# Cutting some stores of an attention gradient into 120 and 8 rows, and 104 and 24 rows

## The chip, the cores and the metric

The kernel runs on one core of one Trainium2 chip. The metric is device time in microseconds for one execution. The profiled execution has a span, from the first to the last instruction of the program, which is a little shorter than its device time.

A core has TensorE (PE in the profile; PEld is its weight load), VectorE (DVE), ScalarE (ACT), GpSimd (POOL) and SyncE (SP), and 16 DMA engines that move data between HBM and the on-chip memory (SBUF, 128 partitions; a partition is called a row below). POOL's and SP's instruction queues issue the DMAs of this kernel.

## What is computed

The reference is the forward pass of a grouped-query attention and its gradients, for B = 32 batches, 32 query heads, 4 key heads, 4 queries, 2048 keys and a head size of 128, in bf16:

```python
scores = jnp.einsum("bhqd,bhkd->bhqk", q, k) * scale
p = _softmax(scores, axis=-1)
return jnp.einsum("bhqk,bhkd->bhqd", p, v)
...
_out, _vjp = jax.vjp(_f, q, k, v)
_grads = _vjp(grad_out)
```

The four outputs are o, dq, dk and dv. k, v, dk and dv are large: 2 MB each for a batch (4 heads x 2048 x 128 values of 2 bytes). q, grad_out, o and dq have 128 x 128 values a batch (32 heads x 4 queries), 32 KB.

## The kernel before

The kernel goes through the 32 batches one at a time, with several in flight. The order of all steps of all engines is written out by hand: a list HEAD for the first batches, a list STEADY of 48 steps that is repeated, and a list TAIL for the last ones. A step such as `dV3@5` is the third eighth of dV of batch 5.

For a batch b, in the order of the data:

- `LK`, `LV` load k and v, four DMAs each of one head (512 KB), from SP's queue. The 2048 keys of a head lie as 128 rows of 16 keys, so that a row of a head is 4 KB in one piece. Three k buffers and two v buffers rotate. Every fourth batch (b % 4 = 3) `LK` also loads q and grad_out of the next four batches, two DMAs of 128 KB from POOL's queue.
- `KT`, `VT`, `QDT` turn k, v, q and grad_out on PE; DVE copies the result out of PSUM.
- `S`, `EX`, `NRM` make scores, exponentials and 1/sum; POOL writes the scaled copies `dop` and `qp` that dV and dK need (line 231).
- `ET` and `O`: o is accumulated on PE, DVE scales it into `o_sb`, and POOL issues its store of 128 rows x 256 bytes. DVE then reads `o_sb` once more for `delta`.
- `dV0` to `dV7`: outer products on PE, ACT copies each eighth into the tile `dv` (128 rows x 4 heads x 16 keys x 128). With the last eighth POOL issues two stores, two heads and 1 MB each.
- `dP`, `dST`, `dQ`, and `dK0` to `dK7`, which are stored as dV is.

The last batch (b = 31) stores dV and dK in another way, by halves of the keys. POOL issues in its queue's order, for each batch: dq, dk, dk (of the batch before), o, dv, dv, and in every fourth the two loads of q and grad_out. `store` in the code is POOL's queue.

DMAs that are issued by POOL take one of eight semaphores in turn. The trace shows them on semaphores 111 to 118 in rotation, and an issue waits until the store that used the semaphore before it has landed.

In the code of before the store of dV and dK is at line 326 (line 319 for the last batch), that of o at line 276, that of dq at line 290, the loads of q and grad_out at line 142, k's and v's at lines 154 and 160.

Of the kernel before, what the change touches and what calls it, by code (L numbers as in the profile page):

```python
# [9 lines left out]
BF16 = mybir.dt.bfloat16  # L10
ACT = mybir.ActivationFunctionType
ALU = mybir.AluOpType
# [69 lines left out]
def kernel(ctx: ExitStack, tc: tile.TileContext, q, k, v, grad_out, out_0, out_1, out_2, out_3):  # L82
    nc = tc.nc
    B, Hq, Sq, D = q.shape
    NH, Sk = k.shape[1], k.shape[2]
    P = 128
# [3 lines left out]
    scale = float(D) ** -0.5  # L90
# [11 lines left out]
    ds_pool = ctx.enter_context(tc.tile_pool(name="dsp", bufs=2))  # L102
    dst_pool = ctx.enter_context(tc.tile_pool(name="dstp", bufs=2))
    out_pool = ctx.enter_context(tc.tile_pool(name="outp", bufs=4))
    io_pool = ctx.enter_context(tc.tile_pool(name="iop", bufs=3))
    qd_pool = ctx.enter_context(tc.tile_pool(name="qdp", bufs=2))
    sm_pool = ctx.enter_context(tc.tile_pool(name="smp", bufs=3))
    ps_pool = ctx.enter_context(tc.tile_pool(name="ps", bufs=1, space=bass.MemoryType.PSUM))
# [16 lines left out]
    o_f = out_0.rearrange("b h s d -> b (h s) d")  # L125
# [6 lines left out]
    store = nc.gpsimd  # L132
    st = {}
# [125 lines left out]
    def gathered(S, xt, kv):  # L259
        t = banks.take(1)  # L260
        ps = banks.ap(t)[:, 0, 0:D]
        for c in range(C):
            for h in range(NH):
                nc.tensor.matmul(  # L264
                    ps[G * h:G * h + G, :], lhsT=S[f"{xt}{c // 8}"][:, c % 8, G * h:G * h + G], rhs=S[kv][:, h, c, :],
                    start=(c == 0), stop=(c == C - 1), tile_position=(0, G * h),
                )
        return t, ps

    def O(b):  # L270
        S = st[b]
        t, ps = gathered(S, "et", "v")
        o_sb = io_pool.tile([P, D], BF16, name="o_sb")
        nc.vector.tensor_scalar(out=o_sb[:], in0=ps, scalar1=S["rinv"][:], scalar2=None, op0=ALU.mult)
        banks.give(t)
        store.dma_start(out=o_f[b], in_=o_sb[:])
        junk = sm_pool.tile([P, D], BF16, name="junk")
        S["delta"] = sm_pool.tile([P, 1], FP32, name="delta")
        nc.vector.tensor_tensor_reduce(
            out=junk[:], in0=o_sb[:], in1=S["do"], scale=1.0, scalar=0.0,  # L280
            op0=ALU.mult, op1=ALU.add, accum_out=S["delta"][:],
        )

# [8 lines left out]
    def outer(S, x, y, dst, name, i, b, copy):  # L292

        if name not in S:
            S[name + "left"] = 8
            S[name] = out_pool.tile([P, NH, C, D], BF16, name=name, tag="outp")
        t = banks.take(2)
        ps = banks.ap(t).rearrange("p a (j c d) -> p a j c d", j=2, c=2)
        for c in range(2):
            u = P * ((2 * i + c) % 8)  # L300
            for a in range(2):
                r = slice(2 * G * a, 2 * G * a + 2 * G)
                nc.tensor.matmul(  # L303
                    ps[:, a, :, c, :], lhsT=S[f"{x}{i // 4}"][r, u:u + P], rhs=S[y][r, :, :],
                    start=True, stop=True, tile_position=(2 * G * a, 0),
                )
        copy(  # L307
            out=S[name][:, :, 2 * i:2 * i + 2, :].rearrange("p h c d -> p h (c d)"),
            in_=banks.ap(t).rearrange("p a (j w) -> p (a j) w", j=2),
        )  # L310
        banks.give(t)
        S[name + "left"] -= 1
        if b == B - 1:

            half = f"{name}half{i // 4}"
            S[half] = S.get(half, 4) - 1
            if S[half] == 0:
                c = slice(8 * (i // 4), 8 * (i // 4) + 8)
                store.dma_start(
                    out=dst[b].rearrange("p h (c d) -> p h c d", d=D)[:, :, c, :].rearrange("p h c d -> p h (c d)"),  # L320
                    in_=S[name][:, :, c, :].rearrange("p h c d -> p h (c d)"),
                )
        elif S[name + "left"] == 0:
            o = S.pop(name)
            for a in range(2):
                store.dma_start(out=dst[b][:, 2 * a:2 * a + 2, :], in_=o[:, 2 * a:2 * a + 2].rearrange("p h c d -> p h (c d)"))  # L326

    def dV(b, i, copy=nc.scalar.copy):
        outer(st[b], "e", "dop", dv_v, "dv", i, b, copy)

    def dK(b, i, copy=nc.scalar.copy):
        outer(st[b], "ds", "qp", dk_v, "dk", i, b, copy)

    def dP(b, i):
# [6 lines left out]
        banks.give(t)  # L341

    table = {"LK": LK, "LV": LV, "QDT": QDT, "O": O, "dQ": dQ, "NRM": NRM}
    for i, c in enumerate("ab"):
        for n, f in (("S", S_), ("EX", EX), ("dP", dP), ("ET", ET), ("dST", dST)):
# [8 lines left out]
    for w in STEADY.split():  # L354
        ahead = 0
        for mark, n in (("+3", 3), ("+2", 2), ("+", 1), ("-2", -2), ("-", -1)):
            if w.endswith(mark):
                w, ahead = w[:-len(mark)], n
# [3 lines left out]
    with tc.manual_schedule():  # L362

        for w in HEAD.split():
            w, b = w.split("@")
# [5 lines left out]
        for w in TAIL.split():  # L371
            w, b = w.split("@")
# [31 lines left out]
```

## Time and profile before

| what | value |
|---|---|
| median of 3 runs | 700.39 us (700.14, 700.39, 703.01) |
| profiled execution | 698.71 us |
| its span | 696.7 us |
| granted TensorE clock, mean | 0.980 |
| PE, DVE, ACT, POOL busy | 90%, 84%, 82%, 43% of the span |
| DMA packets | 75577, 274.44 MB, 394 GB/s over the span |
| POOL's DMA queue (q0), SP's (q1) | 138.16 MB, 134.50 MB |
| issue to landing, median: k, v, dv, dk | 13.8, 18.6, 23.6, 22.1 us |

The DMA share in the profile is the time that packets took, over 16 engines' time. Issue to landing counts from the issuing instruction to the last completion that the transfer sends. A wait in the profile is idle time of an engine, put down to what ended it.

### The profile page before, as it was taken

The numbers are of one execution on the slowest core, as the hardware profiler recorded it, in microseconds if no ns is written. First come the engines' busy times: TensorE is split into PE (matmuls) and PEld (weight loads), VectorE is DVE, ScalarE is ACT, GpSimd is POOL, SyncE is SP. The second block draws the span as 40 slices with busy tenths as digits, with TensorE's granted clock in tenths as the row PEclk, the third lists the DMA queues.
The fourth block names the chain that finished last, engine by engine and source line by source line (L and its number), as shares of the span: only waits on it lengthen the run. The fifth ranks groups of instructions, "written<-read, shape, count | busy, mean of one in ns | idle before, by whom it ended". The sixth has DMA issues, their size and how long they took to land.

```text
span 696.7 us, 28064 instructions
## 1 busy us (share of the span) xinstructions
PE 626.0 (90%) x12352; PEld 454.1 (65%) x12352; DVE 584.5 (84%) x992; ACT 569.1 (82%) x673; POOL 302.7 (43%) x506
## 2 busy tenths in 40 slices
PE   5899999999998989979999798998998889998982
PEld 4577776677676656666666676667766677666661
DVE  5999999999997998869988688888988869898960
ACT  0698989899887989869888687887888868888994
POOL 1355443555454435443354424544434543345452
PEclk9999999999999999999999899999999989999997
DMA  9989999999999999999999999999999999999767
GB/s 339 400 317 411 417 415 416 416 413 415 417 415 417 414 417 416 417 409 412 415 415 413 373 397 398 400 410 382 416 416 417 415 340 393 415 414 415 289 257 274
DMA packets 75577, 274.44 MB, mean 394 GB/s; under 512 B 8448, under 2 KB 8448, under 8 KB 75456
## 3 DMA queue, kind: packets, MB, share of 16 engines
q0 software_dynamic: 37536, 138.16, 49.3%
q1 hardware_dynamic: 37920, 134.50, 48.9%
q8 instruction: 96, 1.57, 0.8%
q14 instruction: 25, 0.20, 0.1%
HBM read 136.31 MB, written 136.31 MB: 391 GB/s over the span
## 4 chain that ended last, share of the span: by engine, by line
PE 43%; DMA 33%; ACT 6%; DVE 5%; POOL 5%; issue 5%; SPq 0%; POOLq 0%; DVEq 0%; ACTq 0%
PE banks L181 18%; DMA k_sb<-in_k_dram 15%; DMA out_dram<-dk 12%; PE banks L303 10%; PE banks L264 7%; ACT dv L307 5%; PE banks L248 5%; DMA out_dram<-dv 4%; PE banks L198 3%; POOL dop L231 2%; DMA v_sb<-in_v_dram 2%; DVE kt L183 2%; DVE ds L338 1%; ACT dk L307 1%; POOL qp L231 1%
## 5 line engine op out<-in xcount | busy, mean ns | idle before, releaser
L307 ACT CAST dv<-banks 128x1024 bf16<-128x1024 f32 x256 | 245.5, 1028 | 56.9 <-PE banks L303 56.3
L307 ACT CAST dk<-banks 128x1024 bf16<-128x1024 f32 x256 | 250.7, 1025 | 34.5 <-PE banks L303 23.6
L183 DVE COPY kt<-banks 128x1024 bf16<-128x1024 bf16 x256 | 164.3, 680 | 8.3 <-PE banks L181 8.3
L183 DVE COPY vt<-banks 128x1024 bf16<-128x1024 bf16 x256 | 166.2, 680 | 1.3 <-PE banks L181 0.9
L181 PE MATMUL banks<-ident,k_sb 128*128 128x128 bf16 x2048 | 145.8, 221 | 13.1 <-DMA k_sb<-in_k_dram 8.6
L181 PE MATMUL banks<-ident,v_sb 128*128 128x128 bf16 x2048 | 143.5, 220 | 14.3 <-ACT dv L307 9.7
L231 POOL TENSOR_SCALAR dop<-do_sb,rinv 32x128 bf16<-32x128 bf16 x128 | 76.7, 599 | 181.3 <-PE banks L303 118.9
L181 PEld LDWEIGHTS <-k_sb 128*128 128x128 bf16 x2048 | 120.8, 99 | 41.9 <-issue 31.7
L181 PEld LDWEIGHTS <-v_sb 128*128 128x128 bf16 x2048 | 122.2, 98 | 28.7 <-issue 23.3
L303 PE MATMUL banks<-dop,e 64*128 64x256 bf16 x1024 | 99.3, 276 | 15.1 <-POOL dop L231 11.3
L326 POOL DMA_DIRECT2D out_dram<-dv x62 | 43.7, 709 | 138.0 <-ACT dv L307 67.6
L338 DVE SCALAR_TENSOR_TENSOR ds<-banks,delta,e 128x1024 bf16<-128x1024 f32 x64 | 82.2, 1284 | 17.3 <-PE banks L198 14.3
L303 PE MATMUL banks<-qp,ds 64*128 64x256 bf16 x1024 | 86.4, 272 | 2.1 <-ACT dk L307 1.4
L231 POOL TENSOR_SCALAR qp<-q_sb,srinv 32x128 bf16<-32x128 bf16 x128 | 78.1, 610 | 10.7
L222 ACT ACTIVATE e<-banks,negb 128x1024 bf16<-128x1024 f32 x64 | 70.7, 1111 | 8.6 <-DVE negb L214 8.5
L211 DVE TENSOR_REDUCE m<-banks 128x1 f32<-128x1024 f32 x64 | 75.1, 1215 | 0.9 <-PE banks L198 0.9
L303 PEld LDWEIGHTS <-e 64*128 64x128 bf16 x1024 | 34.0, 94 | 63.1 <-issue 46.7
L250 DVE COPY et<-banks 128x1024 bf16<-128x1024 bf16 x64 | 41.3, 686 | 29.6 <-PE banks L248 29.6
L303 PEld LDWEIGHTS <-ds 64*128 64x128 bf16 x1024 | 42.2, 94 | 28.8 <-ACT dv L307 13.1
L326 POOL DMA_DIRECT2D out_dram<-dk x62 | 44.0, 713 | 13.6 <-DMA out_dram<-dk 13.0
L250 DVE COPY dst<-banks 128x1024 bf16<-128x1024 bf16 x64 | 43.5, 681 | 5.5 <-PE banks L248 3.6
L248 PE MATMUL banks<-ident,ds 128*128 128x128 bf16 x512 | 39.4, 221 | 7.1 <-ACT dk L307 6.8
(39 smaller groups left out, 484.1 us busy)
## 6 DMA issues: line engine op xcount, KB each, us to landing
k_sb<-in_k_dram SPq DMA_DIRECT2D x128, 512.0 KB, 13.8
v_sb<-in_v_dram SPq DMA_DIRECT2D x128, 512.0 KB, 18.6
out_dram<-dv POOLq DMA_DIRECT2D x64, 1024.0 KB, 23.6
out_dram<-dk POOLq DMA_DIRECT2D x64, 1024.0 KB, 22.1
out_dram<-o_sb POOLq DMA_DIRECT2D x32, 32.0 KB, 23.2
out_dram<-dq_sb POOLq DMA_DIRECT2D x32, 32.0 KB, 16.2
q_sb<-in_q_dram POOLq DMA_DIRECT2D x7, 128.0 KB, 21.9
do_sb<-in_grad_out_dram POOLq DMA_DIRECT2D x7, 128.0 KB, 22.0
```

Of the source, the lines that this page charges most:

```text
L181: nc.tensor.transpose(out=ps[:, 4 * hh + j, :], in_=S[which][:, 2 * (i % 2) + hh, 4 * (i // 2) + j, :], identity=ident[:])
L183: nc.vector.tensor_copy(out=S[f"{which}t{i}"][:], in_=ps)
L211: nc.vector.reduce_max(out=S["m"][:, i:i + 1], in_=S[f"s{i}"][1], axis=AX.X)
L222: nc.scalar.activation(out=S[f"e{i}"][:], in_=ps, func=ACT.Exp, bias=S["negb"][:], scale=scale, accum_out=S["l"][:, i:i + 1],)
L231: nc.gpsimd.tensor_scalar(out=t[r, h % 2, :], in0=src[r, :], scalar1=by[r, :], scalar2=None, op0=ALU.mult)
L248: nc.tensor.transpose(out=ps[:, u, :], in_=S[f"{src}{i}"][:, P * u:P * u + P], identity=ident[:])
L250: nc.vector.tensor_copy(out=S[f"{name}{i}"][:], in_=ps)
L264: nc.tensor.matmul(ps[G * h:G * h + G, :], lhsT=S[f"{xt}{c // 8}"][:, c % 8, G * h:G * h + G], rhs=S[kv][:, h, c, :], start=(c == 0), stop ...
L303: nc.tensor.matmul(ps[:, a, :, c, :], lhsT=S[f"{x}{i // 4}"][r, u:u + P], rhs=S[y][r, :, :], start=True, stop=True, tile_position=(2 * G * ...
L307: copy(out=S[name][:, :, 2 * i:2 * i + 2, :].rearrange("p h c d -> p h (c d)"), in_=banks.ap(t).rearrange("p a (j w) -> p (a j) w", j=2),)
L326: store.dma_start(out=dst[b][:, 2 * a:2 * a + 2, :], in_=o[:, 2 * a:2 * a + 2].rearrange("p h c d -> p h (c d)"))
L338: nc.vector.scalar_tensor_tensor(out=S[f"ds{i}"][:], in0=ps, scalar=S["delta"][:], in1=S[f"e{i}"][:], op0=ALU.subtract, op1=ALU.mult,)
```

## The change

Two stores are cut differently, and one pool of buffers is smaller.

- dV, second store (heads 2 and 3): in the batches with b % 4 = 3 it becomes two, rows 0 to 119 and rows 120 to 127. In batch 0 it becomes three: rows 0 to 119 of head 2, rows 0 to 119 of head 3, rows 120 to 127 of both. The last batch's dV goes another way through the code and stays as it is. dK is not changed.
- o: two batches share one tile. The first four batches, and those with b % 4 = 0 or 1, are stored as before. A batch with b % 4 = 2 issues no store; with b % 4 = 3 both batches are stored, rows 0 to 103 in one DMA and rows 104 to 127 in another.
- the pool of `o_sb` and `dq_sb` has two buffers each in place of three; `o_sb` is twice as large.

All other steps, and their order, are the same. The bytes moved are the same.

```diff
-    io_pool = ctx.enter_context(tc.tile_pool(name="iop", bufs=3))
+    io_pool = ctx.enter_context(tc.tile_pool(name="iop", bufs=2))
...
-        o_sb = io_pool.tile([P, D], BF16, name="o_sb")
-        nc.vector.tensor_scalar(out=o_sb[:], in0=ps, scalar1=S["rinv"][:], scalar2=None, op0=ALU.mult)
-        banks.give(t)
-        store.dma_start(out=o_f[b], in_=o_sb[:])
+        if b % 2 == 0:
+            st["o"] = io_pool.tile([P, 2, D], BF16, name="o_sb")
+        o_sb = st["o"][:, b % 2, :]
+        nc.vector.tensor_scalar(out=o_sb, in0=ps, scalar1=S["rinv"][:], scalar2=None, op0=ALU.mult)
+        banks.give(t)
+        if b < 4 or b % 4 < 2:
+            store.dma_start(out=o_f[b], in_=o_sb)
+        elif b % 4 == 3:
+            for r in (slice(0, 104), slice(104, P)):
+                store.dma_start(out=o_f[b - 1:b + 1, r].rearrange("w p d -> p w d"), in_=st["o"][r])
...
             o = S.pop(name)
             for a in range(2):
-                store.dma_start(out=dst[b][:, 2 * a:2 * a + 2, :], in_=o[:, 2 * a:2 * a + 2].rearrange("p h c d -> p h (c d)"))
+                parts = [(slice(0, P), slice(2 * a, 2 * a + 2))]
+                if name == "dv" and a and b == 0:
+                    parts = [(slice(0, 120), slice(2, 3)), (slice(0, 120), slice(3, 4)), (slice(120, P), slice(2, 4))]
+                elif name == "dv" and a and b % 4 == 3:
+                    parts = [(slice(0, 120), slice(2, 4)), (slice(120, P), slice(2, 4))]
+                for r, h in parts:
+                    store.dma_start(out=dst[b][r, h, :], in_=o[r, h].rearrange("p h c d -> p h (c d)"))
```

## The prediction

> **What bounds the kernel now.** I read the page's busy rows first, then its DMA queues, then the DMA view of single stretches, last POOL's timeline.
>
> ```profile
> span 696.7 us, 28064 instructions
> ...
> PE 626.0 (90%) x12352; PEld 454.1 (65%) x12352; DVE 584.5 (84%) x992; ACT 569.1 (82%) x673; POOL 302.7 (43%) x506
> ...
> DMA  9989999999999999999999999999999999999767
> GB/s 339 400 317 411 417 415 416 416 413 415 417 415 417 414 417 416 417 409 412 415 415 413 373 397 398 400 410 382 416 416 417 415 340 393 415 414 415 289 257 274
> ```
>
> The DMA engines are full from the third slice to the loads' end, at 409 to 417 GB/s as far as slice 22; then dips to 340 appear. PE's 90% is an average that includes waits. The DMA view gives issues, KB each and the median us from issue to landing; here for 60 to 200 us, and below it for 400 to 640 us:
>
> ```profile
> out_dram<-dk POOLq DMA_DIRECT2D x14, 1024.0 KB, 15.9
> out_dram<-dv POOLq DMA_DIRECT2D x14, 1024.0 KB, 21.1
> ```
>
> ```profile
> out_dram<-dk POOLq DMA_DIRECT2D x24, 1024.0 KB, 23.0
> out_dram<-dv POOLq DMA_DIRECT2D x22, 1024.0 KB, 26.1
> ```
>
> The stores fall further behind although the rate doesn't rise. Why, the completions tell. The trace records sixteen for each transfer, one from each DMA engine. Of the second dk store of batch 4, fifteen are in by 143.04 us and the last at 145.00; of batch 16, by 393.39 and at 403.46; of batch 27, by 627.98 and at 642.57. One engine falls behind steadily (2.0, 10.1, 14.6 us). From batch 4 to 16 its pace is (403.46 - 145.00) / 12 = 21.54 us a batch; that of the fifteenth is (393.39 - 143.04) / 12 = 20.86, the mean of all sixteen 20.76. After batch 16 the fifteen are throttled to the late one, which holds its 21.5. When the loads have ended, it is seen alone. In the DMA view of 654 to 657 us:
>
> ```profile
> DMA  0101001001010101010010101010090101010010
> q0 software_dynamic: 15, 0.06, 5.1%
> q8 instruction: 1, 0.02, 2.9%
> q1 hardware_dynamic: 4, 0.01, 1.2%
> ```
>
> 5.1% + 1.2% of sixteen engines is one engine, still at work while fifteen rest. The seventeen 4 KB packets that it starts from 654.10 to 657.02 us are 0.172 us apart; on the others, when busy, packets follow each 0.155 us (34.58 to 36.15 us). So this lane is slow by itself, not by what it is given: all stores of before have 128 rows. An engine's eight rows of two heads are 16 of these packets.
>
> How the lateness comes back shows on POOL's timeline (start, us, instruction; in brackets the idle time before it and what ended that):
>
> ```profile
> 527.09 1.42 POOL L326 DMA_DIRECT2D out_dram<-dk  x2
> 529.95 0.56 POOL L276 DMA_DIRECT2D out_dram<-o_sb  x1 [1.44 <-DMA out_dram<-dk]
> 534.93 1.40 POOL L326 DMA_DIRECT2D out_dram<-dv  x2 [4.42 <-DMA out_dram<-dk]
> 541.85 2.63 POOL L231 TENSOR_SCALAR dop<-do_sb,rinv 32x128 bf16<-32x128 bf16 x4 [5.51 <-PE banks L303]
> ```
>
> Stores rotate over eight semaphores, so each waits for the eighth before it to land in full, its late engine too. These waits throttle fifteen engines; the late one has 14 us of work queued and never rests. Compute alone would go faster: between 73.0 and 191.5 us, before these waits, dv's first store is issued every 19.75 us.
>
> **The change part by part.** The sum is against the profiled execution: 698.71 us, 2.0 more than its span, 1.7 under the median of the three runs (700.39). I carry its differences to the median.
>
> *The dV store cut into 120 and 8 rows.* The bytes stay. No row of before shows how 120 rows are dealt to sixteen engines. If an engine keeps its eight rows, fifteen take part and one is left out; the 8-row piece then gives that engine one row back or none. It loses 14 to 16 packets. If the rows are spread evenly, it loses next to nothing. Which engine is spared, the trace doesn't say either: it doesn't name engines. So one event is worth, if the late lane is the spared one, 14 x 0.172 = 2.4 us at the pace when alone, or 14 x 0.163 = 2.3 at the pace under load (21.54 us less about 0.7 for o, dq, completions and the q and do loads, over 128 packets); with 16 packets, up to 2.75. If another engine is spared, it is worth 0, or -2 x 0.172 = -0.34 where the late lane takes a row of the 8-row piece. I take 2.3. It happens in batches 3, 7, ..., 27: seven times (batch 31 is stored in another way). From batch 3 on the late lane always has a backlog, so a microsecond less of its work is one less at the end: 7 x 2.3 = 16.1. The cap: at 20.86 a batch the fifteenth lane would end 23 x 0.68 = 15.6 us earlier at batch 27, plus the 2.0 it led by at batch 4, so 17.6 at most. The late lane, at 21.54 - 0.58 = 20.96 a batch, stays just the slowest; the seven rows given away cost others 0.08 a batch.
>
> *Whether it is the same engine each time.* If the pieces are dealt from a pointer that runs on, the 120- and 8-row pieces use 15 + 8 shares, o's 104 and 24 rows 13 x 8 and 12 x 2, so 25. Together 48, three times round sixteen: the pointer stands where it stood, and all seven events spare one engine. The first dV's pieces (15 + 15 + 8 = 38) move it by six places once, ahead of the rest. Dealt from a fixed first engine, it is one engine as well.
>
> [...]
>
> *First dV, batch 0.* At 34 us no lane is behind (the sixteenth completion follows the fifteenth by 0.3 us), so no gain. Two more issues of 0.71 us are followed by an idle POOL: its next store is at 47.3 us. Cost 0.
>
> *o in pairs.* In batch b%4 = 2 the issue (0.56 us) goes, in b%4 = 3 there are two; the store of the even batch moves past two dv, one dq and two dk stores of POOL's queue. Nobody reads o on the chip except DVE, from SBUF. An engine's share is 2 KB of a batch, one packet of 0.08 us; whatever the dealing does, it is under 0.2 us an event, either way. I take 0.
>
> *One more dV issue in every fourth batch.* 0.71 us of POOL in front of the next dop. POOL waits 5.51 us for PE there: hidden. Without that cover it would be 7 x 0.71 = 5.0 us. The wait for the eighth store back is a rival below.
>
> *io pool with two buffers.* dq_sb is written again two batches later, 42 us; its store lands 16.2 us (median) after issue. An o pair is written again four batches later. 0, and a landing over 40 us would be needed for more.
>
> [...] Here the 32 KB o stores already run among full queues at 415 GB/s without a dip.
>
> Sum: 698.71 - 16.1 = 682.6 in a profiled execution, 684.3 in the median.
>
> **Rivals.** *Another engine is spared, or the rows are spread evenly.* For: nothing in the trace ties the late lane to rows 120 to 127. Against: the pieces close on one engine every time, and the late engine is also one and the same throughout. Times: 700.4, or 700.4 + 7 x 0.34 = 702.8 where the late lane takes one of the eight rows. Both are within 0.5% (3.5 us), about what a measurement of this kernel can tell from no change. In this case the change doesn't do what it could.
>
> *Slower: POOL's wait for the eighth store back.* In a batch with b%4 = 3 the order becomes dq, dk, dk, o, o, dv, dv, dv. The last piece then waits for the last dv store of the batch before: in the timeline above that one (issued at 514.4) lands at 545.9, so POOL would be held until then and not until 536.3. dop, ready to start at 541.85, would start 4.8 us late, and PE with its dV. Price without cover: 7 x 4.8 = 33.6, so 734. Against it: compute has (21.5 - 19.75) x 4 = 7 us to spare in four batches, and the late lane keeps its backlog of 14 us. It decides only if the hold in four batches exceeds these 7 us, say by a slow issue of odd pieces on POOL; with 2 us over, 7 x 2 = 14 and 714. If the late lane is relieved, the wait shrinks with the landing.
>
> *No engine has what the late one lost.* If the fifteenth lane becomes the bound early (cap halved), the gain is about 8: 692.
>
> **How the numbers follow.** Late lane spared, in full: 0.47, 680 to 688. Spared but capped: 0.11, 688 to 696. Another engine or even spread: 0.33, 699 to 703.5. POOL's wait: 0.09, 704 and up. The first is a judgement, as the trace doesn't name engines; I put it over the miss because the spared engine is one and the same by the arithmetic, as the late lane is throughout, and because the rows left over are always the last eight. If the two places are unrelated, a hit is one in sixteen and the miss is the answer; that doubt is the 0.33. Faster by over 0.5%: 0.58; within: 0.33; slower: 0.09. Range 680 to 703.5, which leaves out POOL's wait; the likeliest case alone is 680 to 688.
>
> **What would show it.** Right: the sixteenth completion of batch 27's second dk store is a few us behind the fifteenth, not 14.6; landing of dk and dv at 400 to 640 us near 17 to 20 us; POOL's 4.4 us waits gone or shorter; GB/s near 415 with few dips. Miss: the same 14 us and the same landing medians. POOL's wait: three dv issues with a gap of 5 us or more before the last, and dop released by POOL, with PE idle. Wrong altogether: time and landings both move, but no lane's lag does.

## The result, and the profile after

Over twenty runs of each kernel the changed one takes 702.60 us (700.32 to 706.26) and the one before 700.38 (698.19 to 703.40): ratio 1.0031, 95% interval 1.0019 to 1.0042. The change brings nothing and costs some 2 us. The profiled execution of after took 703.15 us, 4.4 more than that of before.

The first fence is the head of the profile page of after: span, DMA share and rate in 40 slices.

```profile
span 701.3 us, 28111 instructions
...
DMA  8999999999999999999999999999999999999867
GB/s 336 398 316 404 414 414 411 415 414 416 415 416 415 411 416 412 414 391 407 414 385 404 403 416 413 358 411 387 400 409 364 408 408 400 396 386 416 337 237 266
```

The dips from the middle of the run on are still there (391, 385, 358, 387, 364). The DMA view of after for 400 to 640 us (issues, KB each, median us from issue to landing) shows the two pieces of dV apart:

```profile
out_dram<-dk POOLq DMA_DIRECT2D x24, 1024.0 KB, 21.5
...
out_dram<-dv POOLq DMA_DIRECT2D x19, 1024.0 KB, 24.4
out_dram<-dv POOLq DMA_DIRECT2D x3, 960.0 KB, 26.5
...
out_dram<-dv POOLq DMA_DIRECT2D x3, 64.0 KB, 21.8
```

dk and dv land 1.5 and 1.7 us sooner than before, not down to the forecast's 17 to 20 us, and a store of 8 rows takes 21.8 us, nearly as long as one of 128. The completions say why. Of the second dk store of batch 27, the sixteenth was in at 642.57 us before and is at 642.50 after: the late engine has been relieved of nothing. The fifteenth moved from 627.98 to 634.52. The lag of the late engine is 8.0 us in place of 14.6 only because the other fifteen are slower; the lag alone would have passed for half a success.

What holds the other fifteen shows in POOL's waits. Three groups of the wait view (engine and line, what it waited for, us in total, times, longest us), of before and then of after:

```profile
POOL dop L231 <- PE banks L303: 118.9, 20, 6.6
POOL out_dram L326 <- DMA out_dram<-dv: 22.1, 6, 4.2
PE banks L303 <- POOL dop L231: 11.3, 11, 2.4
```

```profile
POOL dop L231 <- PE banks L309: 93.5, 19, 6.2
POOL out_dram L340 <- DMA out_dram<-dv: 72.5, 22, 4.5
PE banks L309 <- POOL dop L231: 21.2, 16, 2.9
```

POOL waits 50 us more for landed dv stores and 25 us less for PE; PE waits 10 us more for `dop`. In a batch with the cut, POOL's timeline of after (start, us, instruction; in brackets the idle time before it and what ended it) reads:

```profile
430.62 0.73 POOL L340 DMA_DIRECT2D out_dram<-dv  x1 [4.99 <-DMA out_dram<-dk]
435.17 0.74 POOL L340 DMA_DIRECT2D out_dram<-dv  x1 [3.82 <-DMA out_dram<-dv]
440.44 0.55 POOL L340 DMA_DIRECT2D out_dram<-dv  x1 [4.53 <-DVE vt L183]
441.08 2.63 POOL L231 TENSOR_SCALAR dop<-do_sb,rinv 32x128 bf16<-32x128 bf16 x4
```

Each dv piece now waits on its own, and `dop` follows the last issue with no pause: POOL is no longer waiting for PE there. The stores eight back, on the same semaphores, had their last completions at 430.06, 434.89 and 440.16 us, each 0.3 to 0.6 us before the issue that waited. (DVE's vt as what ended the last wait is a neighbour in time; DVE gives nothing to that store.)

### The profile page after: what moved, and what is told of

Read it like the earlier page. It is cut to its first block, busy times and chain, and to the rows that moved or that the text cites. A ratio compares the mean times of both kernels' runs of the same rounds, so it can differ in the third digit from the quotient of the medians.

```text
span 701.3 us, 28111 instructions
## 1 busy us (share of the span) xinstructions
PE 629.5 (90%) x12352; PEld 457.5 (65%) x12352; DVE 584.0 (83%) x992; ACT 569.4 (81%) x673; POOL 309.8 (44%) x515
## 4 chain that ended last, share of the span: by engine, by line
PE 51%; DMA 23%; issue 8%; ACT 6%; POOL 6%; DVE 4%; SPq 0%; POOLq 0%; ACTq 0%; DVEq 0%
PE banks L181 21%; DMA out_dram<-dv 14%; PE banks L309 13%; PE banks L264 7%; DMA out_dram<-dk 7%; PE banks L248 5%; ACT dv L313 5%; PE banks L198 4%; POOL dop L231 3%; DMA v_sb<-in_v_dram 2%; POOL out_dram L340 2%; DVE kt L183 1%; DVE ds L352 1%; ACT dk L313 1%; DMA k_sb<-in_k_dram 1%
## 5 line engine op out<-in xcount | busy, mean ns | idle before, releaser
L340 POOL DMA_DIRECT2D out_dram<-dv x71 | 49.1, 693 | 176.8 <-ACT dv L313 76.2
L309 PE MATMUL banks<-dop,e 64*128 64x256 bf16 x1024 | 101.2, 277 | 24.8 <-POOL dop L231 21.2
L309 PE MATMUL banks<-qp,ds 64*128 64x256 bf16 x1024 | 88.8, 273 | 2.1 <-ACT dk L313 1.4
L309 PEld LDWEIGHTS <-ds 64*128 64x128 bf16 x1024 | 44.2, 94 | 28.8 <-ACT dv L313 12.7
L276 DVE TENSOR_SCALAR o_sb<-banks,rinv 128x128 bf16<-128x128 f32 x32 | 11.2, 351 | 39.8 <-PE banks L264 39.2
```

The costliest lines, as they stand in the source:

```text
L309: nc.tensor.matmul(ps[:, a, :, c, :], lhsT=S[f"{x}{i // 4}"][r, u:u + P], rhs=S[y][r, :, :], start=True, stop=True, tile_position=(2 * G * ...
L340: store.dma_start(out=dst[b][r, h, :], in_=o[r, h].rearrange("p h c d -> p h (c d)"))
```

## How the dealing can be read

The trace names no engine, but it shows one that is left out: an engine that gets no rows of a POOL store still moves very small packets. Packets of POOL's queue, by size in bytes:

```
before: 4 x3296, 2048 x1024, 4096 x33216
after:  4 x3696, 16 x28, 64 x21, 1024 x84, 2048 x800, 4096 x33307
```

The change adds, in seven pairs of o, 7 x 13 = 91 packets of 4096 bytes and 7 x 3 = 21 of 64 (104 rows on 13 engines, 3 left out), 7 x 12 = 84 of 1024 and 7 x 4 = 28 of 16 (24 rows on 12 engines, 4 left out). So 16 - k engines are left out where a store is dealt to k. For a 120-row dV store the left-out engine shows a chain of sixteen and more 4-byte packets, 5.9 ns apart. In after one of them starts at 437.25 us, while that store's completions run from 437.86 to 461.7: the left-out engine stands at the front, so it is a fast one. The 4-byte packets tell how many are left out there. In before they are as many as the completions on POOL's eight semaphores, 206 x 16 = 3296; after has 215 x 16 = 3440 completions and 256 such packets more. In seven events, 15 engines for 120 rows leave one out, with 16 packets, and 8 for 8 rows leave eight out, with 2 each: 7 x (16 + 8 x 2) = 224, and 224 of the 256 come after 70 us. The other 32 are of batch 0.

When the 64-byte packets of a 104-row store come late, with its last completion, the late engine is among the three left out. Where it lies, and where it doesn't, in kernels with different dealing tells its place. Below, places 0 to 15 are counted from the engine where the program's dealing begins. That a store which is dealt to k engines, k under 16, moves the place where the next such store begins by k is an assumption, which the runs below test, and the turn is the number of places by which batch 0 has moved it. For 104, 24, 120 and 8 rows k is that of the packets above (13, 12, 15 and 8); for the other cuts below (22 rows on 11 engines, say) it is an estimate after these, where the engines that take part get equal rows. Then, as counted, the 120-row store leaves out place (turn + 15) mod 16, and its 8-row piece gives a row of each head to eight places from that one on. The first event leaves the place 15 + 8 = 23 further on, so the 104-row store takes thirteen places from turn + 7 on and leaves out turn + 4, + 5 and + 6. The 24-row store behind it leaves out turn to turn + 3, and its 16-byte packets tell of these four in the same way.

## The experiments

The diffs are against the changed kernel, except where said. The timed ratio is to the kernel before, on the same chip; "late end" is the sixteenth completion of batch 27's second dk store (before 642.57, after 642.50). It is that of one execution: in e3, which stores dV as before, it is 644.28, so differences of less than 2 us say little.

**No cut of the first dV (e1).**

```diff
-                if name == "dv" and a and b == 0:
-                    parts = [(slice(0, 120), slice(2, 3)), (slice(0, 120), slice(3, 4)), (slice(120, P), slice(2, 4))]
-                elif name == "dv" and a and b % 4 == 3:
+                if name == "dv" and a and b % 4 == 3:
```

> The changed kernel without the cut of the first dV store; all else as changed. In the changed kernel's trace the engine that each 120-row store leaves out is one that finishes among the first, and the late lane keeps all its packets (batch 27's second dk store ends at 642.50, before the change at 642.57). Theory A, one running pointer decides which engine is left out and the cut of the first dV only turns it by six places: now another engine is left out, the same in all seven events. If that is the late lane: about 684 us, lag of the sixteenth completion at batch 27 a few us. If it is again another one: 700 to 703, lag 8 to 14 us. Theory B, the engine left out is fixed by the row order and the first dV has no say: 702.6, same lane left out as in the changed kernel.

703.92 us, 1.005 (1.0018 to 1.0083); late end 644.60. A 64-byte packet of a 104-row store comes at 451.08 us with that store's last completion at 451.8, the other fifteen being in by 439.3. Without a turn the late engine is among the three left out there, as counted at place 4, 5 or 6, and it gets a row of each 8-row piece. In after no such packet comes late (for the same pair the last is at 437.10 us, the store's last completion at 451.24): the first dV's pieces do turn the dealing, but not to the right place.

**The same stores, dealt evenly (e2)** (112 and 16 rows for 120 and 8, 64 and 64 for 104 and 24).

```diff
-                parts = [(slice(0, 120), slice(2, 4)), (slice(120, P), slice(2, 4))]
+                parts = [(slice(0, 112), slice(2, 4)), (slice(112, P), slice(2, 4))]
```

> The changed kernel with the same number of stores, cut so that the rows can be dealt evenly over sixteen engines: dV as 112 and 16 rows, o pairs as 64 and 64. Theory A, what the change lost (2.2 us) comes from the extra stores and POOL's waits for the eighth store back: 702 to 703, the wait of 4 to 5 us before the last dV piece stays. Theory B, it comes from the dealing itself, extra rows on some lanes: 700.4, as before the change.

702.88 us, 1.002 (1.0005 to 1.0036); late end 643.04. As slow as after, with no engine left out: packets under 512 bytes at 400 to 640 us are 2598, in before 2605, in after 2715. The same two waits as in after:

```profile
POOL out_dram L340 <- DMA out_dram<-dv: 60.0, 19, 4.5
PE banks L309 <- POOL dop L231: 21.8, 19, 2.1
```

So the 2 us go with the extra stores, and the uneven rows of after are worth nothing.

**Only o changed (e3)**, dV stored as before.

```diff
-                if name == "dv" and a and b == 0:
-                    parts = [(slice(0, 120), slice(2, 3)), (slice(0, 120), slice(3, 4)), (slice(120, P), slice(2, 4))]
-                elif name == "dv" and a and b % 4 == 3:
-                    parts = [(slice(0, 120), slice(2, 4)), (slice(120, P), slice(2, 4))]
```

> Only the o part of the change (pairs as 104 and 24 rows, two buffers); dV is stored as before. Theory A (the loss comes from the ninth dV piece and the wait in front of it): 700.4, no difference. Rival (the loss comes from the o pairs, whose two stores stand in front of dV in POOL's queue): about 702.6.

700.57 us, 0.9999 (0.9987 to 1.0012). The pairs of o and the smaller pool cost nothing. With the run above, dV's additional stores (two in batch 0, seven later) cost 702.88 - 700.57 = 2.3 us by the medians, 1.7 by the means.

This run's packets tell the place as well. As counted, its dealing begins at place 0, and each pair of o moves it by 13 + 12 = 25, nine over sixteen, so the engines left out change from pair to pair. A 16-byte packet comes late with the second pair (275.86 us, last completion 276.48) and with the fourth (448.91, 449.53), none before the last pair with the others. As counted, the 24-row stores of these two pairs leave out places 2 to 5 and 4 to 7, and the other four leave out neither 4 nor 5: the late engine is at place 4 or 5.

**A load cut instead (e4)**: in the kernel before, v of head 3 in odd batches as 120 and 8 rows, from SP's queue.

```diff
-            nc.sync.dma_start(out=S["v"][:, h].rearrange("p c d -> p (c d)"), in_=v_v[b, h])
+            for r in (slice(0, 120), slice(120, P)) if h == 3 and b % 2 else (slice(0, P),):
+                nc.sync.dma_start(out=S["v"][r, h].rearrange("p c d -> p (c d)"), in_=v_v[b, h, r])
```

> The kernel before, with no store cut; instead one load of v (head 3) in every second batch is cut into 120 and 8 rows, from SP's queue. Theory A, the late lane is the one that gets the last eight rows of a load, and a 120-row load from SP always leaves that one out: it loses 8 packets of 0.163 us in 14 batches from batch 4 on, 18 us, so 682 to 686, and the lag at batch 27 is a few us. Rival, the late lane is not the one with the last rows or another engine is left out: 700.4 or, with one row more on the late lane in 14 batches (14 x 0.163 = 2.3), 702.7; lag 14 us as before.

703.11 us, 1.0028 (1.0013 to 1.0043); late end 643.04. Sixteen cuts take nothing off the late engine, and one completion of an 8-row load comes up to 14 us behind its others (of the load issued at 601.60 us, at 621.0, the others by 607.3). So the cuts on SP's queue don't spare the late engine; that it is one of those that get a row of the 8-row loads is the author's reading of that completion.

**A turn by five, with single-head pieces of the first dV (e5).**

```diff
-                if name == "dv" and a and b == 0:
-                    parts = [(slice(0, 120), slice(2, 3)), (slice(0, 120), slice(3, 4)), (slice(120, P), slice(2, 4))]
-                elif name == "dv" and a and b % 4 == 3:
+                if name == "dv" and b == 0:
+                    parts = [
+                        [(slice(0, P), slice(0, 1)), (slice(0, 120), slice(1, 2))],
+                        [(slice(0, 120), slice(2, 3)), (slice(0, 120), slice(3, 4)), (slice(120, P), slice(1, 4))],
+                    ][a]
+                elif name == "dv" and a and b % 4 == 3:
```

> The changed kernel with the pieces of the first dV chosen so that the pointer is turned by five places (15 + 15 + 15 + 8 = 53) instead of six. In e1 (no turn) the late lane is one of the three that the 104-row store leaves out, so four to six places on from the pointer; in the changed kernel (six more) it is left out of no piece, which leaves only the place four on. A turn of five makes each 120-row store leave out exactly that lane. Theory A, running pointer and late lane is the bound: 684 us (680 to 689), no backlog of 8 to 14 us at batch 27, landing of dv and dk at 400 to 640 us under 22 us. Rival 1, the pointer isn't what places the left-out engine, or the late lane changes from launch to launch: 701 to 704. Rival 2, the late lane is relieved but the others bound, or POOL's waits do: lag gone, time 692 to 700.

702.92 us, 1.0023 (1.0009 to 1.0037); late end 642.96. The late engine is neither left out nor given a row, just as in after. By 15 + 15 + 15 + 8 = 53 the place should have moved by 5 and the late engine been spared; it wasn't.

**The same turn, with the cut in every second batch (e6).**

```diff
-        if b < 4 or b % 4 < 2:
+        if b < 4:
...
-        elif b % 4 == 3:
+        elif b % 2 == 1:
...
-                elif name == "dv" and a and b % 4 == 3:
+                elif name == "dv" and a and b % 2 == 1 and b >= 3:
```

> As e5, but dV is cut in every second batch from 3 on, and o pairs (104 and 24 rows) are stored in every second batch from 5 on, so that the pointer comes round in two batches. The late lane loses twice as much, 1.16 us a batch where it lags 0.68. Theory A: the other fifteen lanes bound, 681 to 684, slightly better than e5. Rival, POOL's waits for the eighth store back come twice as often and eat it: slower than e5 by 2 us or more. If the late lane isn't hit: 703 to 706.

705.70 us, 1.0062 (1.0041 to 1.0084); late end 641.38, the fifteenth at 639.77. Twice the cuts cost more and still don't spare the late engine. Its lag falls to 1.6 us because the others are held.

**The turn by o of the first three batches (e7)** (120 and 8 rows each, 3 x 23 = 69, five over 64), no cut of the first dV.

```diff
-        if b < 4 or b % 4 < 2:
+        if b < 3:
+            for r in (slice(0, 120), slice(120, P)):
+                store.dma_start(out=o_f[b, r], in_=o_sb[r])
+        elif b < 4 or b % 4 < 2:
```

> As e5, but the pointer is turned by the tiny o stores: o of batches 0, 1 and 2 is cut into 120 and 8 rows each (3 x 23 = 69, which is five over four rounds of sixteen), and the first dV is stored whole halves. Theory A, only the sum of the places counts: the same time as e5 within 0.3%. Rival, the first dV's cut matters by itself: another time than e5.

705.77 us, 1.0055 (1.0031 to 1.008). The late engine is among the 104-row store's left-outs again, as with no turn at all. Six pieces that should have moved the place didn't.

**The turn of e5 with fewer stores (e8)**: o of b % 4 = 0 and 1 in one store of 128 rows.

```diff
-        if b < 4 or b % 4 < 2:
+        if b < 4:
...
+        elif b % 4 == 1:
+            store.dma_start(out=o_f[b - 1:b + 1].rearrange("w p d -> p w d"), in_=st["o"][:])
```

> As e5, but o of the batches with b % 4 = 0 and 1 is stored as a pair too, in one store of 128 rows, from batch 4 on: 26 stores and loads on POOL's queue in four batches, as before the change, and not 27. Theory A, the late lane bounds: the same as e5 within 1 us. Rival, with the lane relieved POOL's waits count: faster than e5 by 1 to 3 us.

702.42 us, 1.0025 (1.0008 to 1.0041), against 702.92 of e5 on the same chip: the intervals overlap, so seven stores fewer show no gain here.

**Four turns by o of batch 0 (e9 to e12)**: 96, 22 and 10 rows, or 96 with 20 and 12, 18 and 14, 24 and 8, undone by dq of batches 29 and 30, also cut, so that an execution would end where it began. The first dV isn't cut. The part of e9's edit that makes the turn:

```diff
-        if b < 4 or b % 4 < 2:
+        if b == 0:
+            for r in (slice(0, 96), slice(96, 118), slice(118, 128)):
+                store.dma_start(out=o_f[b, r], in_=o_sb[r])
+        elif b < 4 or b % 4 < 2:
```

> e5 and e7 turn the pointer by the same five places, and yet in their profiles the late lane stands elsewhere against the pieces. Theory A: the pointer isn't set back between executions, and each execution of e5 and e7 moves it on by five (of the changed kernel by six). Here the turn of five is made by o of batch 0 (96, 22 and 10 rows: 16 + 11 + 10 = 37) and is undone by dq of batches 29 and 30 (11 places), so that an execution leaves the pointer where it found it. dV and the o pairs are cut as in the changed kernel. If the pointer then starts where it did for e1 and e3 (no net turn before them; there the late lane was four or five places on), this kernel leaves out the place four on: 684 us (680 to 690) in every run if that is the late lane, else 701 to 705. Rival: the late lane changes from launch to launch; then this and the next three agree on no place.

> As e9, with a turn of six, undone by ten: the place five on is left out. It is the changed kernel's own turn, undone at the end. By theory A one of e9 and e10 is at about 684 us and the other at 701 to 705; with the late lane of neither, both at 701 to 705 and the profile shows where it is. Rival as for e9.

> As e9, with a turn of seven, undone by nine: the place six on is left out. By theory A 701 to 705 if the late lane is four or five on. Its profile gives a third reading of the place, and all three have to agree; by the rival they don't.

> As e9, with a turn of four, undone by twelve: the place three on is left out. By theory A 701 to 705, and 703 to 705 when the late lane takes one of the eight rows (places three to ten on).

705.25 (1.0059, 1.0038 to 1.0079), 705.28 (1.0078, 1.0053 to 1.0103), 703.74 (1.0055, 1.0036 to 1.0075) and 704.46 us (1.0065, 1.0038 to 1.0092); late ends 645.02, 644.69, 644.89 and 646.38. All four are the kernel without a turn: 64-byte packets at 451.0, 450.7, 450.8 and 451.8 us, each within 0.9 us of the last completion. The theory that every piece moves the place had failed in eight kernels (e5 to e12). What the pieces without effect have in common is that each is one contiguous block of HBM (rows of one head, or of one batch's o). The pieces that do turn have two or three heads or two batches, so they are strided. By this rule the first dV of the change turns by 8 alone, its last piece, and e5's does too.

**Turns by two-head pieces only (e13 and e14).** If that rule holds, the first dV in strided pieces turns as counted: 16 + 10 + 12 = 38, so 6, and 16 + 11 + 10 = 37, so 5.

```diff
-                    parts = [(slice(0, 120), slice(2, 3)), (slice(0, 120), slice(3, 4)), (slice(120, P), slice(2, 4))]
+                    parts = [(slice(0, 96), slice(2, 4)), (slice(96, 116), slice(2, 4)), (slice(116, 128), slice(2, 4))]
```

```diff
-                    parts = [(slice(0, 120), slice(2, 3)), (slice(0, 120), slice(3, 4)), (slice(120, P), slice(2, 4))]
+                    parts = [(slice(0, 96), slice(2, 4)), (slice(96, 118), slice(2, 4)), (slice(118, 128), slice(2, 4))]
```

> The changed kernel with the first dV's second half cut into 96, 20 and 12 rows, each of two heads, in place of two single-head pieces of 120 rows and one of 8. Theory A (only pieces that are strided in HBM, two heads or two batches, move the place at which the next store's rows are dealt; single-head and single-batch pieces do not): the three pieces take 16 + 10 + 12 = 38 engines, the place moves by 6, and the 120-row store of every fourth batch leaves out the sixth engine from the start. If that is the late one, the lag of the sixteenth completion at batch 27's second dk store falls from about 11 to some 14 us to under 6 and the time is 680 to 690 us; if the late one is its neighbour, which gets a row of the 8-row piece, 702 to 706. Theory B (the first turn is of no consequence, or the spared packets are worth nothing, because POOL's waits set the pace): 701 to 704 us, whatever engine is left out, with the late lane's end at batch 27 within 1 us of 642.5.

> The same with 96, 22 and 10 rows of two heads each: 16 + 11 + 10 = 37 engines, so the place moves by 5, and the 120-row store leaves out the fifth engine from the start. Theory A: one of the two kernels of this call leaves out the late engine and takes 680 to 690 us, the other, where the late engine gets a row of each 8-row piece, 702 to 706 us. Theory B: 701 to 704 us for both. If the late engine is spared and the time still stays over 698 us, the spared packets are not what the time hangs on.

Turned by 6: 702.44 us, 1.0024 (1.0008 to 1.004), late end 642.80. Turned by 5: **690.60 us**, 0.9849 (0.9833 to 0.9866), late end 628.16, 1.6 us behind the fifteenth. The page of the latter:

```profile
span 688.5 us, 28111 instructions
...
DMA  9989999999999999999999999999999999999967
GB/s 336 408 302 407 415 416 416 415 414 416 416 414 416 414 416 415 416 415 416 417 414 415 410 414 417 409 404 408 416 414 404 408 406 413 411 395 416 364 244 262
```

and its DMA view for 400 to 640 us:

```profile
out_dram<-dk POOLq DMA_DIRECT2D x23, 1024.0 KB, 20.3
...
out_dram<-dv POOLq DMA_DIRECT2D x21, 1024.0 KB, 23.8
```

The lowest slice between the fifth and the thirty-fifth is now 404 GB/s; it was 340 before and 358 in after. The same rows 96, 22 and 10 that did nothing as one batch's o spare the late engine as two heads of dV. A neighbouring place (turn 6) is worth nothing. POOL's own waits for dv are nearly those of after, but PE no longer pays for them:

```profile
POOL out_dram L340 <- DMA out_dram<-dv: 69.3, 21, 5.4
...
PE banks L309 <- POOL dop L231: 10.8, 12, 1.3
```

**One place further back, more often, and with fewer stores**, all by two-head pieces: 96, 24 and 8 rows (16 + 12 + 8 = 36, turn 4; e17); the turn of 5 with the cuts of e6 (e16); the turn of 5 with the o pairs of e8 (e15). The diff is that of e17, against e14.

```diff
-                    parts = [(slice(0, 96), slice(2, 4)), (slice(96, 118), slice(2, 4)), (slice(118, 128), slice(2, 4))]
+                    parts = [(slice(0, 96), slice(2, 4)), (slice(96, 120), slice(2, 4)), (slice(120, 128), slice(2, 4))]
```

> The first dV's second half as 96, 24 and 8 rows of two heads: 16 + 12 + 8 = 36 engines, so the place moves by 4 and the 120-row store leaves out the engine just before the one that the turn of 5 spared, while the 8-row piece starts with that engine and takes in the next seven. Theory A (the late engine is the one that the turn of 5 spared): it now gets a row of every 8-row piece, and the time is that of no turn at all, 703 to 706 us, with the late lane's end at batch 27 at 644 to 646 us. Rival (the turn of 5 is fast for another reason, such as the three pieces themselves or their shapes): 690 to 692 us here too.

> The turn of 5, with dV cut and o paired in every second batch in place of every fourth: 14 events in place of 7, each worth 2.3 us of the late engine. Theory A (after the first seven events the late engine is level with the others, so there is nothing left to take, and each extra store costs POOL): 690 to 694 us. Rival (the late engine still sets the pace after seven events): 682 to 688 us, with its lag at batch 27 negative, that is, hidden among the others.

> The turn of 5, and o of batches b%4 = 0 and 1 (from batch 4 on) stored at once as 128 rows: seven stores fewer, so that POOL issues as many as before the change. Theory A (two microseconds per execution came from the extra stores' waits when nothing was spared): 688.5 to 691 us. Rival (with the late engine spared these waits no longer bind): the same as with the turn of 5 alone, within 0.5 us of 690.6.

Turn 4: 705.98 us, 1.0075 (1.0049 to 1.0102), late end 645.12. This fits a late engine at place 4, the one that a turn of 5 leaves out and that now gets a row of every 8-row piece. The packets agree: a 16-byte one comes at 452.46 us (last completion 453.18), and as counted the 24-row stores leave out places 4 to 7 here. Cut in every second batch: 693.31 us, 0.9908 (0.9883 to 0.9933); late and fifteenth completions are level (629.38 and 628.52), nothing is left to take, and the extra stores cost. With the useless turn the same number of cuts took 705.70. Fewer stores: **689.25 us**, 0.9841 (0.9815 to 0.9866), faster than both kernels of this study; against the turn of 5 alone the intervals overlap, so the part of the fewer stores isn't shown.

**Half the events (e18)**: e15 with dV cut in batches 3, 11, 19 and 27 only, and o as 104 and 24 rows in 7, 15, 23 and 31.

```diff
-        elif b % 4 == 1:
+        elif b % 4 == 1 or b % 8 == 3:
...
-                elif name == "dv" and a and b % 4 == 3:
+                elif name == "dv" and a and b % 8 == 3:
```

> The turn of 5 with o pairs as one store, and dV cut in every eighth batch only (batches 3, 11, 19, 27; o as 104 and 24 rows in 7, 15, 23, 31): four events in place of seven, so the late engine is relieved of 4 x 2.4 = 9.6 us and not 16.8. Theory A (the late engine's backlog costs only from where it throttles the others, so the first part of the relief takes little and each event counts alike until it is level): seven events brought 9.8 to 11 us, so four bring about 6, 693 to 696 us, with a lag of 6 to 9 us at batch 27. Rival (only a backlog over some size costs, and half the relief already keeps it under that): 688.5 to 691.5 us, as with all seven.

692.80 us, 0.9883 (0.9862 to 0.9904), late end 633.76, lag 4.9. That lies just below the first theory's 693 to 696 and above the rival's 691.5: four events bring 7.5 us of the 10.4 that seven bring. In proportion it would be 5.9. Whether the first events count for more isn't shown: the intervals of the two gains allow proportion, and e18 issues six stores fewer than e15.

All turns together, counted by the rule that only strided pieces turn:

| turn | left out | gets a row of 8 | kernels | late end | us |
|---|---|---|---|---|---|
| 0 | 15 | 15, 0 to 6 | e1, e7, e9 to e12 | 642.7 to 646.4 | 703.7 to 705.8 |
| 8 | 7 | 7 to 14 | after, e5, e8 | 642.5 to 644.0 | 702.4 to 702.9 |
| 6 | 5 | 5 to 12 | e13 | 642.8 | 702.4 |
| 4 | 3 | 3 to 10 | e17 | 645.1 | 706.0 |
| 5 | 4 | 4 to 11 | e14, e15 | 628.2, 626.9 | 690.6, 689.3 |

Place 4 as the late one fits every row but the late end of e7 (642.67, the one profile without a turn that isn't clearly later than before). Where place 4 is left out, the row it gets back from the 8-row piece is already in its saving. The kernels ran on five chips. On two of them (e13 and e14; e15 to e18) the turns single out place 4; on the others the late packets leave 4 or 5 (e1 and e3) and 4 to 6 (e7; e9 to e12). The four runs of e14 lie within 690.39 to 690.90, though each execution moves the place by 5 in total; so every execution seems to begin anew.

## Why the prediction failed, point by point

**What bounds the kernel: right.** One DMA engine is late (14.6 us behind the fifteenth at batch 27 in before) and throttles the rest (the mean completion moves on by 20.76 us a batch from batch 4 to 16 and by 21.59 from there to 27). Packets taken off it made the kernel 1.5% faster (turn of 5, 690.60 us), packets taken off its neighbour nothing (turn of 6, 702.44 us).

**Which engine is spared: the step that failed.** The forecast of 684.3 rested on "if the late lane is the spared one", with 0.58 on it in two cases, although the trace of before named no engine. The spared one was a fast one (place 7 as counted), the late one is at place 4. That both are one and the same throughout is no reason that they are the same; the text's own "one in sixteen" was the honest figure, and the rival with 0.33 is what happened.

**How far the first dV turns: wrong.** "15 + 15 + 8 = 38" counted single-head pieces that don't move the place; by the rule that the runs left, the turn was 8, not 6. It decided nothing: the run with a true turn of 6 took 702.44 us. That the events close on the same engine (48) was right: all four pieces there are strided, and in e14 the late engine's lag stays at 2.1 us or less to the end.

The shares in the sum of 48 (15, 8, 13 and 12) are those of after's packets. For strided pieces the runs agree with a place that moves by as many: turned by 5 the late end is 628.16 us, by 4 and by 6 it is 645.12 and 642.80. Pieces that are contiguous in HBM left the place where it was (e9 to e12, 644.69 to 646.38 us). The turn of 38 counted all pieces alike.

**What an event is worth: right for the engine, too large for the time.** For the late engine, seven events were put at 16.1 us; its end at batch 27 came 642.57 - 628.16 = 14.4 us earlier in e14, by when it was level with the others, and 642.57 - 633.76 = 8.8 after the four events of e18, 2.2 each. The row too many was put at 0.34 an event, 2.4 in all; e17, with as many stores as e13 and such a row, has a ratio of 1.0075 against 1.0024, about 3.6 us, and the intervals include 2.4. But "a microsecond less of its work is one less at the end" is mis-sized: the medians gained 9.8 us (e14) and 10.4 (e15). The mean of the sixteen completions of each second dk store shows where (us a batch):

| kernel | batches 4 to 16 | batches 16 to 27 | mean completion at 27 |
|---|---|---|---|
| before | 20.76 | 21.59 | 628.08 |
| after | 21.03 | 21.63 | 633.17 |
| turn 5 (e14) | 20.85 | 20.89 | 622.42 |
| turn 5, fewer stores (e15) | 20.82 | 20.86 | 621.65 |
| turn 5, half the events (e18) | 20.74 | 21.08 | 624.04 |

Up to batch 16 the late engine's backlog grows to 10 us in before and slows nobody; there is nothing to gain there (mean completion 390.64 us, and 392.59 in e14). Only then does it throttle the rest. From batch 16 to 27 that costs 11 x (21.59 - 20.76) = 9.1 us, of which e14 gets 11 x (21.59 - 20.89) = 7.7 back. From 27 to 30 it gains 3.0 more, so that its lead in mean completion is 5.7 us at batch 27, 8.7 at batch 30 and 8.2 in the span. The last of the backlog need not be taken off: in before it is 14.6 us at batch 27 and 0.7 at batch 30. The forecast had 20.76 and the sentence "after batch 16 the fifteen are throttled", but its cap of 17.6 was taken from the late engine's own lag, over all batches. e18 fits: four events keep the backlog at 3.5 us at batch 16 and 4.9 at batch 27, and most of the throttling is gone. From the last v load (issued at 633.56 us before, 624.61 in e14, 8.9 earlier) to the end both take about the same, 63.1 and 63.9 us. By which way the late engine throttles, late loads or POOL's waits, no run separates.

**o in pairs, the smaller pool: right**, 0 (e3).

**One more dV issue: "hidden" was wrong by some 2 us** (e2 less e3). The cover was the 5.5 us that POOL waited for PE; the piece waits nearly that long for its semaphore (4.53 us in after's timeline) and uses the cover up. The rival of POOL's wait named this mechanism and priced it at 33.6 without cover; its sign (gaps between three dv issues, `dop` behind the last) is in the timeline, its price was about a fifteenth. That the batches in between make up for it, having time to spare, is likely but no run isolates it. In the table the loss comes early: from batch 4 to 16 after loses 12 x (21.03 - 20.76) = 3.2 us, and e14, with as many stores but the late engine level with the others, 12 x (20.85 - 20.76) = 1.1. So 702.8, which the text gives for a late engine that gets a row more, comes near the measured 702.60 by luck: in after the late end didn't move.

**What would show it**: "the same 14 us" as the sign of a miss misled. The lag fell to 8.0 by the others' delay. The completion's own time, 642.57 against 642.50, was the sign to name.

## What to carry to other kernels

When a change helps one resource out of sixteen, ask first what ties that resource to the one the change touches; if the trace doesn't say, the chance is the share, not the neatness of the scheme. Read the lag of the slowest against its absolute time, since a lag also shrinks when everything else gets slower. And price a backlog by the pace of the whole with and without it, stretch by stretch: here it cost nothing while it grew to 10 us, and the last of it was worked off at the end without help.

## What the hardware showed that was not expected

- In these runs POOL's stores moved the dealing place only where their HBM side was strided. Rows 96, 22 and 10 of one batch's o left it where it was (705.25 us), the same rows of two heads moved it by 5 (690.60 us). Strided meant two or three heads or two batches in every case; no other kind was run.
- As far as the four runs of e14 tell (690.39 to 690.90 us), the dealing starts at the same place in every execution. As counted, the slow engine is the fifth from there on two chips, and on three more the packets allow the same. Which of the sixteen place 0 is wasn't shown.
- An engine without rows is not silent: in after a 104-row store leaves three 64-byte packets (21 for seven stores), a 24-row one four of 16 bytes (28 for seven). They make the dealing visible in a trace that names no engine.
